# Two units of a Strassen-type product by turns in eight banks, with side work in small steps

## The chip, the cores and the metric

The kernel runs on one core of one Trainium2 chip. The metric is the device time of one execution in microseconds (us): the median of the runs.

## What is computed

```python
def _attn_ref(q_l, k_l, v_l, q_g, k_g, v_g):      # 4 sequences, 8 heads, 512 local + 32 global rows, 64 wide
    ...                                           # sliding-window attention with global rows
def _moe_ref(x, w_in, w_out):                     # 2304 x 512, hidden 2048
    h = np.maximum(x @ w_in, 0.0)
    return (h * h @ w_out).astype(np.float32)
def _moe2_ref(x, w1, w2, w3, w_out):              # hidden 1024
    a = x @ w1
    b = x @ w2
    h = a * b @ w3
    return (h @ w_out).astype(np.float32)
def reference(...):
    x = attn_out.transpose(0, 2, 1, 3).reshape(B * S, H * D)
    x = _moe_ref(x=x, **moe_kwargs)
    return _moe2_ref(x=x, **moe2_kwargs)
```

## The kernel before

Activations lie transposed: 128 partitions hold a slice of the 512 features, and the rows of the four sequences (p = 0 to 3, 544 rows each) lie along the free side. Precision comes from splitting each float32 operand in a high and a low part (`split_operand`, `split_w`: a cast on ScalarE to the high part, a subtraction on DVE for the low one) and from three matmuls (`PASSES`) for each product. ScalarE is called ACT and GpSimd POOL in the rows, DMA issues go by SP's queue.

Attention and the first MLP come first, in blocks of 256 or 288 rows; beside them the weights are converted from their 64-bit form (`conv`). The second MLP multiplies w3 by w_out once into one matrix of 1024 x 512 (`w_unit`, stored to `w_d`), so that two products are left.

The *first product* (the stage of the change) is a and b and their elementwise product, `ab_unit(p, f)`: a unit takes 128 hidden columns of w1 together with those of w2 as two block rows (a above, b below), the two halves of the 512 inputs as the inner blocks, and the two halves of a sequence's rows (272 each, `NP`) as block columns. This 2 x 2 block product is done with seven products in place of eight (Winograd's form, `ORDER` = 1, 6, 5, 7, 4, 2, 3). Each product is six matmuls of 272 columns (two inner blocks, three passes), so a unit is 42 and the 32 units are 1344. `Blocks.step(i)` issues product i (L709) and the operations that read its bank: after product 1 a copy by ScalarE (L726), after 6, 7, 4 and 3 additions by DVE (L729, 731, 733, 736, 739); `ab_unit.done` adds the elementwise product (L845 on DVE after product 2, L847 on GpSimd after 3). Products 7, 2 and 3 accumulate onto the banks of 6, 1 and 5 (`BANK`). A unit takes four of the eight PSUM banks, so the units alternate between two sets.

f = 4 h + j: the units j and 4 + j give slice j of the two halves of the hidden layer, which are the inner blocks of the last product; they share a staging tile `rs` (two buffers), in which GpSimd makes the sums that the last product needs (L848, one for h = 0, three for h = 1), and which goes to DRAM (`q_d`, L856).

The operands of a sequence come from `load_x2` (one load), four subtractions of 544 columns (L754) and 14 splits (L745 cast, L119 subtraction) in `operands`. The tile ring for them has seven places of two and one from the ring `u1`, so one operand of the next sequence can lie ready while the old ones are in use. They are issued for units 4 and 6 and then between the products of a sequence's last unit.

The weights of units FIRST are split when they are converted; the sums and values of those of LATE go to DRAM and come back (`late_w12`, 16 casts at L414 and 16 subtractions at L119), and are then kept in ring `u2` up to the last sequence, which begins with them. There the combined matrix Wv takes their place (`load_wv`, `late_blocks`); its sums are made by GpSimd in the second sequence (`sum_wv`). The *last product*, `y_unit(p, s)`, runs two units by turns, each product being 12 matmuls; its rows are read back from `q_d` (`load_r`, L893) and split (`split_r`).

The order of the instructions of each engine is made by a scheduler when the program is built: an instruction that is traced later may be placed ahead of an earlier one of the same engine, where its inputs and buffers allow it. `tc.keep_in_program_order(i)` ties i behind what was traced before it on its engine. `merge` spreads lists of steps over others.

Of the kernel before, what the change touches and what calls it, by code (L numbers as in the profile page):

```python
# [74 lines left out]
NP = S // 2  # L75

# [8 lines left out]
def attention_mlp(ctx: ExitStack, tc: tile.TileContext, kq0, kq, vw, wts, mask, ident, out_d):  # L85
    nc = tc.nc
# [326 lines left out]
    def split_w(t, cols, raw):  # L413
        nc.scalar.copy(t[:, 0, cols], raw)  # L414
        split_lo(nc.vector, t[:, 1, cols], raw, t[:, 0, cols])
# [15 lines left out]
    def split_blocks(key, n, x, s, tag):  # L431

        p, q, r = (unit(tag) for _ in range(3))
        split_w(p, slice(0, 512), x[:, 0])
        split_w(q, slice(0, 512), s[:, 0])
        split_w(r, slice(0, 512), s[:, 1])
        if n % 2 == 0:
            half_t[tag] = unit(tag)
        h, at = half_t[tag], 256 * (n % 2)
        split_w(h, slice(at, at + 256), x[:, 1, 256:])  # L440
        blocks_w[key] = {1: (p, 0), 2: (p, 256), 5: (q, 0), 6: (q, 256), 7: (r, 0), 3: (r, 256), 4: (h, at)}

    def conv_c(n):
        _, b, m = mid_t.pop(n)
        if n >= PAIRED:
# [4 lines left out]
            if u == 1:  # L450
# [5 lines left out]
                else:  # L456
                    split_blocks(FIRST[k - 4], k, x, s, "u1")
# [286 lines left out]
    def split_operand(t, raw):  # L744
        nc.scalar.copy(t[:, 0], raw)  # L745
        split_lo(nc.vector, t[:, 1], raw, t[:, 0])
        return t

    def operands(p, x, t1, t2):
# [3 lines left out]
        def make(i):  # L753
            sub = lambda o, a, c: nc.vector.tensor_tensor(out=o, in0=a, in1=c, op=ALU.subtract)  # L754
            if i == 0:
                sub(t1, b(0, 1), b(0, 0))
                sub(t2, b(1, 1), t1)
                return
            if i == 7:
                sub(t1, b(1, 1), b(0, 1))  # L760
            if i == 4:
                sub(t2, t2, b(1, 0))
            raw = {1: b(0, 0), 6: t2, 5: t1, 7: t1, 4: t2, 2: b(1, 0), 3: b(1, 1)}[i]
            spare = (7 * p + ORDER.index(i)) % 8 == 7
            xo["x", p, i] = [
                split_operand(unit("u1")[:, :, :NP] if spare else parts(NP), raw[:, k]) for k in range(2)
            ]

        return {i: lambda i=i: make(i) for i in (0, *ORDER)}
# [26 lines left out]
    def ops_early(d):  # L796
        if d == 0:
            first_ops()
            ops[0][0]()
        if d < 2:  # L800
            ops[0][ORDER[d]]()
# [18 lines left out]
    main += [lambda i=i: ops[0][i]() for i in ORDER[2:]] + [end]  # L820
# [5 lines left out]
    stage = {}  # L826

    def ab_unit(p, f):
# [7 lines left out]
        def out(m, n):  # L836
            if (m, n) == (1, 1):
# [189 lines left out]
```

## Time and profile before

| | us |
|---|---|
| median of 3 runs | 905.8 (905.39 to 906.59) |
| profiled execution | 909.1 |
| its span | 907.3 |
| PE busy in it | 853.8 (94%) |
| DVE busy | 589.8 (65%) |
| ScalarE busy | 493.6 (54%) |
| GpSimd busy | 209.0 (23%) |
| first product (L709) on PE from | 615.8 |

PE's busy time is that of matmuls, whose ends are modelled; "idle before" is the time in which an engine had nothing to run ahead of that row, with what ended it. A row of a timeline merges like instructions that follow one another. PEclk is the granted clock of TensorE as a share of full speed, 2.4 GHz.

### The profile page before, as it was taken

The numbers are of one execution on the slowest core, as the hardware profiler recorded it, in microseconds if no ns is written. First come the engines' busy times: TensorE is split into PE (matmuls) and PEld (weight loads), VectorE is DVE, ScalarE is ACT, GpSimd is POOL, SyncE is SP. The second block draws the span as 40 slices with busy tenths as digits, with TensorE's granted clock in tenths as the row PEclk, the third lists the DMA queues.
The fourth block names the chain that finished last, engine by engine and source line by source line (L and its number), as shares of the span: only waits on it lengthen the run. The fifth ranks groups of instructions, "written<-read, shape, count | busy, mean of one in ns | idle before, by whom it ended". The sixth has DMA issues, their size and how long they took to land.

```text
span 907.3 us, 17924 instructions
## 1 busy us (share of the span) xinstructions
PE 853.8 (94%) x6664; PEld 802.3 (88%) x6664; DVE 589.8 (65%) x1617; ACT 493.6 (54%) x1317; POOL 209.0 (23%) x254
## 2 busy tenths in 40 slices
PE   5799999999999999899998999999989998989998
PEld 3578898899999999899898998998979898889998
DVE  6998775876576465456444346898484847677762
ACT  6886675766576577777555446775020203234550
POOL 1432000000010022222222112210754443442000
PEclk9889999999999999999999999999999998999999
DMA  6743525133232156466454549576473333637762
GB/s 231 242 156 102 170 62 156 53 124 100 97 120 74 48 182 206 156 226 204 147 188 139 187 162 326 190 241 228 150 243 111 112 107 103 222 126 256 250 231 74
DMA packets 85303, 147.51 MB, mean 163 GB/s; under 512 B 6112, under 2 KB 58464, under 8 KB 85216
## 3 DMA queue, kind: packets, MB, share of 16 engines
q1 hardware_dynamic: 85216, 146.37, 49.0%
q8 instruction: 52, 0.85, 0.4%
q14 instruction: 35, 0.29, 0.1%
HBM read 100.07 MB, written 46.27 MB: 161 GB/s over the span
## 4 chain that ended last, share of the span: by engine, by line
PE 47%; DMA 20%; DVE 16%; ACT 11%; issue 4%; SPq 1%; POOL 1%; ACTq 0%; DVEq 0%; POOLq 0%
PE m L709 16%; DMA wraw<-in_wts 11%; PE h L130 10%; PE x L130 7%; DMA rl<-q_d 4%; PE o L124 3%; DVE hl L119 3%; DVE u L119 3%; DVE wt L404 3%; PE sc L124 3%; PE tp L278 3%; PE acc L539 2%; ACT wt L391 2%; ACT u L414 2%; DMA x2l<-x_d 2%
## 5 line engine op out<-in xcount | busy, mean ns | idle before, releaser
L130 PE MATMUL h<-hl,u 128*128 128x288 f32 (+1 forms) x1536 | 232.1, 295 | 7.0 <-ACT r L503 3.1
L130 PEld LDWEIGHTS h<-hl,u 128*128 128x128 f32 x1536 | 206.9, 191 | 15.3 <-ACT r L503 5.5
L709 PE MATMUL m<-hl,u 128*128 128x272 f32 x1488 | 202.8, 294 | 14.1 <-DVE r L731 6.1
L709 PEld LDWEIGHTS m<-hl,u 128*128 128x128 f32 x1488 | 194.9, 193 | 17.8 <-DVE r L731 7.2
L539 PE MATMUL acc<-hl,u 128*128 128x256 f32 (+1 forms) x960 | 138.9, 290 | 3.1 <-ACT hl L504 1.7
L539 PEld LDWEIGHTS acc<-hl,u 128*128 128x128 f32 x960 | 128.8, 190 | 6.1 <-DVE hl L119 2.4
L459 POOL TENSOR_TENSOR wt<-wt 128x512 int32<-128x512 int32 x56 | 76.2, 1361 | 227.9 <-DVE wt L404 132.0
L119 DVE TENSOR_TENSOR hl<-r,hl 128x288 fp32r<-128x288 f32 (+1 forms) x128 | 65.5, 519 | 63.0 <-ACT r L510 62.6
L130 PE MATMUL x<-hl,u 128*128 128x288 f32 (+1 forms) x576 | 89.2, 297 | 0.2 <-ACT u L414 0.2
L391 ACT ACTIVATE wt<-wraw 128x512 f32<-128x512 f32 x72 | 48.3, 673 | 63.0 <-DMA wraw<-in_wts 62.5
L130 PEld LDWEIGHTS x<-hl,u 128*128 128x128 f32 x576 | 76.9, 189 | 4.5 <-issue 1.9
L709 PE MATMUL m<-u,u 128*128 128x272 f32 x528 | 73.9, 289 | 4.1 <-DVE r L729 2.2
L709 PEld LDWEIGHTS m<-u,u 128*128 128x128 f32 x528 | 68.2, 188 | 6.2 <-DVE r L729 2.6
L201 ACT ACTIVATE p<-p,st 128x256 f32<-128x256 f32 x128 | 64.2, 506 | 9.9 <-DVE st L197 9.8
L119 DVE TENSOR_TENSOR u<-wt,u 128x512 fp32r<-128x512 f32 x56 | 39.8, 712 | 44.3 <-ACT u L414 43.6
L503 ACT ACTIVATE r<-h 128x288 f32<-128x288 f32 (+1 forms) x128 | 49.5, 391 | 32.9 <-PE h L130 32.3
L726 ACT COPY r<-m 128x272 f32<-128x272 f32 x40 | 15.3, 383 | 81.3 <-PE m L709 62.3
L197 DVE CUSTOM_DVE_ANT_0 p<-sc,mask_sb 128x256 f32<-128x256 f32 x128 | 46.9, 417 | 19.1 <-PE sc L124 18.9
L230 POOL CAST qgp<-kq_hl 64x32 fp32r<-64x32 f32 x48 | 16.4, 343 | 178.1 <-PE sg L130 149.8
L404 DVE SCALAR_TENSOR_TENSOR wt<-wraw,wt 128x512 int32<-128x512 int32 x72 | 54.5, 756 | 1.4
L504 ACT ACTIVATE hl<-r 128x288 fp32r<-128x288 f32 (+1 forms) x128 | 54.0, 430 | 2.0
L848 POOL TENSOR_TENSOR rs<-rs 128x272 f32<-128x272 f32 x64 | 52.8, 835 | 3.3
(97 smaller groups left out, 1203.5 us busy)
## 6 DMA issues: line engine op xcount, KB each, us to landing
wraw<-in_wts SPq DMA_DIRECT2D x72, 512.0 KB, 3.7
q_d<-rs SPq DMA_DIRECT2D x16, 952.0 KB, 4.5
rl<-q_d SPq DMA_DIRECT2D x12, 1088.0 KB, 5.7
v_f<-in_vw SPq DMA_DIRECT2D x24, 256.0 KB, 3.0
xs_d<-hl SPq DMA_DIRECT2D x16, 288.0 KB, 3.2
hl<-xs_d SPq DMA_DIRECT2D x16, 288.0 KB, 4.0
x2l<-x_d SPq DMA_DIRECT2D x4, 1088.0 KB, 7.5
out<-u SPq DMA_DIRECT2D x16, 272.0 KB, 3.4
```

What stands on the lines that cost most here:

```text
L119: eng.tensor_tensor(out=lo, in0=raw, in1=hi.bitcast(F32), op=ALU.subtract)
L124: m = mm(o, w, x, start=start, stop=stop)
L130: mm(o, w, x, start=(k == 0), stop=(k == len(terms) - 1))
L201: nc.scalar.activation(p[:, n, :], p[:, n, :], AF.Exp, bias=least[:, n : n + 1], scale=-1.0, accum_out=sums[:, n, 0:1],)
L391: first = nc.scalar.activation(t[0].bitcast(F32), raw[:, :, 1].bitcast(F32), AF.Copy, scale=2.0**-112)
L404: nc.vector.scalar_tensor_tensor(out=b, in0=raw[:, :, 1], scalar=-(1 << 31), in1=a, op0=ALU.bitwise_and, op1=ALU.bitwise_or)
L459: nc.gpsimd.tensor_tensor(out=b, in0=b, in1=m, op=ALU.add)
L503: nc.scalar.activation(r, h, AF.Relu)
L504: nc.scalar.activation(g[:, 0], r, AF.Square)
L539: mm(acc[d], w[:, a, 128 * d : 128 * (d + 1)], g_t[f][:, b], start=(f + k == 0), stop=(f + k == 9),)
L709: mm(o, w, x, start=(i in (1, 6, 5, 4) and k == 0), stop=(k == len(terms) - 1), skip_group_check=(i in (2, 7, 3)),)
L848: sub = lambda o, a, c: nc.gpsimd.tensor_tensor(out=o, in0=a, in1=c, op=ALU.subtract)
```

## The change

Two units (0 and 4, 1 and 5, 2 and 6, 3 and 7 of a sequence, in the same order of pairs) run product by product by turns: product 1 of both, then 6 of both, and so on. Between the products of a pair `between(p, m, k)` issues the side work in fixed small steps, by tables: AHEAD (steps of the next sequence's operands by pair m and product k), LATE_W and LATE_V (steps of the late weights in the first and of Wv in the last sequence). The DVE subtractions of the splits and the operands' subtractions (from the second sequence on) are tied to program order. The operands get ten places, two of them from the ring `xb`. The third result of a unit goes to the staging tile instead of a temporary; the stores to `q_d` are issued three products into the next pair. Loads for the last product are issued earlier and use `rs` buffers too. Of the diff, lines without change are left out.

```diff
@@ -73,6 +73,14 @@
+PLACES = 10
+AHEAD = ((0, 0, 0, 0, 0, 0, 0), (1, 0, 1, 0, 1, 0, 1), (1, 0, 1, 0, 1, 0, 1), (2, 1, 2, 0, 2, 1, 2))
+LATE_W = ((2, 1, 1, 0, 2, 1, 1), (1, 1, 1, 1, 1, 1, 1), (1, 1, 1, 0, 1, 0, 0))
+LATE_V = ((1, 0, 0, 0, 0, 0, 0), (2, 1, 2, 0, 2, 1, 1), (2, 1, 2, 0, 2, 1, 2), (0, 0, 0, 0, 0, 0, 0))
@@ -410,9 +418,13 @@
     def unit(tag, dtype=F32R):
-    def split_w(t, cols, raw):
+    def split_w(t, cols, raw, held=False):
-        split_lo(nc.vector, t[:, 1, cols], raw, t[:, 0, cols])
+        s = nc.vector.tensor_tensor(
+            out=t[:, 1, cols], in0=raw, in1=t[:, 0, cols].bitcast(F32), op=ALU.subtract
+        )
+        if held:
+            tc.keep_in_program_order(s)
@@ -428,17 +440,22 @@
-    def split_blocks(key, n, x, s, tag):
-        p, q, r = (unit(tag) for _ in range(3))
-        split_w(p, slice(0, 512), x[:, 0])
-        split_w(q, slice(0, 512), s[:, 0])
-        split_w(r, slice(0, 512), s[:, 1])
-        if n % 2 == 0:
-            half_t[tag] = unit(tag)
-        h, at = half_t[tag], 256 * (n % 2)
-        split_w(h, slice(at, at + 256), x[:, 1, 256:])
-        blocks_w[key] = {1: (p, 0), 2: (p, 256), 5: (q, 0), 6: (q, 256), 7: (r, 0), 3: (r, 256), 4: (h, at)}
+    def split_blocks(key, n, x, s, tag, held=False):
+        t = []
+        def third(raw):
+            t.append(unit(tag))
+            split_w(t[-1], slice(0, 512), raw, held)
+        def last():
+            if n % 2 == 0:
+                half_t[tag] = unit(tag)
+            (p, q, r), h, at = t, half_t[tag], 256 * (n % 2)
+            split_w(h, slice(at, at + 256), x[:, 1, 256:], held)
+            blocks_w[key] = {1: (p, 0), 2: (p, 256), 5: (q, 0), 6: (q, 256), 7: (r, 0), 3: (r, 256), 4: (h, at)}
+        return [*(lambda raw=raw: third(raw) for raw in (x[:, 0], s[:, 0], s[:, 1])), last]
     def conv_c(n):
@@ -454,7 +471,8 @@
-                    split_blocks(FIRST[k - 4], k, x, s, "u1")
+                    for f in split_blocks(FIRST[k - 4], k, x, s, "u1"):
+                        f()
@@ -741,32 +759,53 @@
-    def split_operand(t, raw):
+    def split_operand(t, raw, held=True):
-        split_lo(nc.vector, t[:, 1], raw, t[:, 0])
+        s = nc.vector.tensor_tensor(out=t[:, 1], in0=raw, in1=t[:, 0].bitcast(F32), op=ALU.subtract)
+        if held:
+            tc.keep_in_program_order(s)
+    room = {}
+    def place(n):
+        n, at = divmod(n, PLACES)
+        if at < 7:
+            return [parts(NP) for _ in range(2)]
+        if at == 7:
+            return [
+                unit("u1").rearrange("p a c -> p (a c)")[:, : 2 * NP].rearrange("p (a c) -> p a c", a=2)
+                for _ in range(2)
+            ]
+        if at == 8:
+            room[0] = sb.tile([128, 2, 2, 2, NP], F32R, tag="xb", name="xo", bufs=2)
+        return [room[0][:, at - 8, k] for k in range(2)]
     def operands(p, x, t1, t2):
-        def make(i):
-            sub = lambda o, a, c: nc.vector.tensor_tensor(out=o, in0=a, in1=c, op=ALU.subtract)
-            if i == 0:
-                sub(t1, b(0, 1), b(0, 0))
-                sub(t2, b(1, 1), t1)
-                return
+        def sub(o, a, c):
+            s = nc.vector.tensor_tensor(out=o, in0=a, in1=c, op=ALU.subtract)
+            if p > 0:
+                tc.keep_in_program_order(s)
+        raw = {1: b(0, 0), 6: t2, 5: t1, 7: t1, 4: t2, 2: b(1, 0), 3: b(1, 1)}
+        def split(i, k):
+            if k == 0:
+                xo["x", p, i] = place(7 * p + ORDER.index(i))
+            split_operand(xo["x", p, i][k], raw[i][:, k], p > 0)
+        steps = [lambda: sub(t1, b(0, 1), b(0, 0)), lambda: sub(t2, b(1, 1), t1)]
+        for i in ORDER:
-                sub(t1, b(1, 1), b(0, 1))
+                steps.append(lambda: sub(t1, b(1, 1), b(0, 1)))
-                sub(t2, t2, b(1, 0))
-            raw = {1: b(0, 0), 6: t2, 5: t1, 7: t1, 4: t2, 2: b(1, 0), 3: b(1, 1)}[i]
-            spare = (7 * p + ORDER.index(i)) % 8 == 7
-            xo["x", p, i] = [
-                split_operand(unit("u1")[:, :, :NP] if spare else parts(NP), raw[:, k]) for k in range(2)
-            ]
-        return {i: lambda i=i: make(i) for i in (0, *ORDER)}
+                steps.append(lambda: sub(t2, t2, b(1, 0)))
+            steps += [lambda i=i, k=k: split(i, k) for k in range(2)]
+        return steps
     def in_staging():
@@ -796,9 +835,8 @@
     def ops_early(d):
-            ops[0][0]()
-        if d < 2:
-            ops[0][ORDER[d]]()
+        for _ in range(4 if d == 0 else 2 if d == 1 else 0):
+            ops[0].pop(0)()
@@ -817,13 +855,18 @@
-    main += [lambda i=i: ops[0][i]() for i in ORDER[2:]] + [end]
+    main += [lambda n=n: [ops[0].pop(0)() for _ in range(n)] for n in (2, 3, 3, 2, 2)] + [end]
-    stage = {}
+    stage, made = {}, []
+    def store_r():
+        for p, j in made:
+            nc.sync.dma_start(out=q_d[:, :, p, j], in_=stage[p, j][:, 1:])
+        made.clear()
     def ab_unit(p, f):
@@ -834,11 +877,9 @@
         def out(m, n):
-            if (m, n) == (1, 1):
-                return temp()
-            return stage[p, j][:, (1, 0, 6, 7)[2 * h + n]]
+            return stage[p, j][:, ((1, 0, 2), (6, 7, 5))[h][n + m * n]]
         def done(u, i):
@@ -853,7 +894,7 @@
-                    nc.sync.dma_start(out=q_d[:, :, p, j], in_=stage[p, j][:, 1:])
+                    made.append((p, j))
@@ -868,17 +909,35 @@
     def sum_wv(j):
-        nc.sync.dma_start(out=sums_d[4 + j], in_=add_up(load_wv(j), "u2", nc.gpsimd))
-    def late_blocks(key, n, x):
-        s = unit("u2", F32)
-        nc.sync.dma_start(out=s, in_=sums_d[n])
-        split_blocks(key, n, x, s, "u2")
-    def late_w12(k):
+        sums = add_up(load_wv(j), "u2", nc.gpsimd)
+        return lambda: nc.sync.dma_start(out=sums_d[4 + j], in_=sums)
+    late_t = {}
+    def late_load(key, n, load):
+        late_t[n] = (load(), unit("u2", F32))
+        nc.sync.dma_start(out=late_t[n][1], in_=sums_d[n])
+    def late_split(key, n, k):
+        if k == 0:
+            late_t[n] = split_blocks(key, n, *late_t[n], "u2", True)
+        late_t[n][k]()
+    def load_w12(k):
-        late_blocks(LATE[k], k, x)
+        return x
+    def late_steps(todo, order=(0, 1, None, 2, None, 3, None, None)):
+        load = [lambda t=t: late_load(*t) for t in todo]
+        steps, n = [], 0
+        for k in order:
+            if k is not None:
+                steps.append(load[k])
+                continue
+            steps += [lambda t=todo[n], k=k: late_split(*t[:2], k) for k in range(4)]
+            n += 1
+        return steps
     def next_x(p):
@@ -889,7 +948,11 @@
     def load_r(p, o):
-            t = sb.tile([128, 2, 4, NP], F32, tag="xb", name="rl", bufs=2)[:, :n]
+            if o < 4:
+                t = sb.tile([128, 2, 4, NP], F32, tag="xb", name="rl", bufs=2)[:, :n]
+            else:
+                t = rs.tile([128, 8, NP], F32, tag="rs", name="rl", bufs=2)
+                t = t.rearrange("p (k j) n -> p k j n", k=2)[:, :n]
@@ -905,37 +968,51 @@
+    late_v = late_steps([(("v", j), 4 + j, lambda j=j: load_wv(j)) for j in range(4)], (0, 1, None, None, 2, 3, None, None))
+    late_w = late_steps([(LATE[k], k, lambda k=k: load_w12(k)) for k in range(4)])
+    def take(steps, n):
+        for f in steps[:n]:
+            f()
+        del steps[:n]
+    def between(p, m, k):
+        if k == 3:
+            store_r()
+            take(sums_v, len(sums_v))
+        if p + 1 < B:
+            if m == 0 and k == 0:
+                next_x(p + 1)
+            take(ops[p + 1], AHEAD[m][k])
+            if p == 0 and m < 3:
+                take(late_w, LATE_W[m][k])
+        else:
+            if m == 2 and k in (0, 3):
+                load_r(0, 2 * k // 3)
+            take(late_v, LATE_V[m][k])
+            if m == 3 and k in (1, 4):
+                split_r(0, ORDER[k // 4])
+        if p == 1 and k == 0:
+            sums_v.append(sum_wv(m))
+    sums_v = []
+    late_w.pop(0)()
     for p in range(B):
-        for n, f in enumerate(order):
-            box = []
-            if n == 1:
-                main.append(lambda p=p: next_x(p + 1))
-            if n in (4, 6) and p + 1 < B:
-                main.append(lambda p=p, i=(0, 1)[n // 5]: ops[p + 1][i]())
-            if p == 1 and n % 2 == 0:
-                main.append(lambda j=n // 2: sum_wv(j))
-            if p == B - 1 and n in (2, 3, 4, 5):
-                main.append(lambda j=n - 2: late_blocks(("v", j), 4 + j, load_wv(j)))
-            if p == B - 1 and n == 4:
-                main.append(lambda: load_r(0, 0))
-            if p == B - 1 and n == 6:
-                main.append(lambda: split_r(0, 1))
-            if p == B - 1 and n == 7:
-                main.append(lambda: split_r(0, 6))
-            for i in ORDER:
-                if i == 1:
-                    main.append(lambda box=box, p=p, f=f: (box.append(ab_unit(p, f)), box[0].step(1)))
-                else:
-                    main.append(lambda box=box, i=i: box[0].step(i))
-                if n == 7 and p + 1 < B and i != 3:
-                    main.append(lambda p=p, i=ORDER[ORDER.index(i) + 1]: ops[p + 1][i]())
-            if p == B - 1 and n == 7:
-                for o in (2, 4, 6):
-                    main.append(lambda o=o: load_r(0, o))
-                    for i in ORDER[o : o + 2]:
-                        main.append(lambda i=i: split_r(0, i))
-    merge(main, ([lambda k=k: late_w12(k) for k in range(4)], 0, 30))
+        for m in range(4):
+            units = [ab_unit(p, f) for f in order[2 * m : 2 * m + 2]]
+            for k, i in enumerate(ORDER):
+                for u in units:
+                    u.step(i)
+                between(p, m, k)
+    store_r()
+    for o in (4, 6):
+        load_r(0, o)
+    for i in ORDER[2:]:
+        split_r(0, i)
+    for o in (0, 2, 4, 6):
+        load_r(1, o)
     def y_unit(p, s):
@@ -969,9 +1046,9 @@
-            if o % 2 == 0:
-                load_r(p + 1, o)
+            if o in (1, 3, 5, 6):
+                load_r(p + 2, o - o % 2)
```

## Rows read from the trace of the kernel before

**Rows 1.** Busy time by stretch; columns: window, length, each engine's busy us (operations), PEclk, DMA.

```profile
622.00:640.00 18.00, 16.14 (x123) 15.33 (x122) 14.25 (x33) 5.37 (x15) 5.87 (x8) 1.00 0.64 225
656.00:676.00 20.00, 16.01 (x124) 15.33 (x123) 18.21 (x36) 6.31 (x17) 11.97 (x15) 1.00 0.68 214
706.00:722.00 16.00, 14.25 (x105) 13.26 (x105) 15.21 (x33) 5.32 (x16) 6.13 (x7) 1.00 0.30 99
751.00:773.00 22.00, 19.02 (x130) 18.66 (x129) 17.07 (x36) 7.77 (x19) 7.73 (x9) 0.84 0.28 96
773.00:812.00 39.00, 34.00 (x241) 33.18 (x240) 25.91 (x57) 11.93 (x27) 14.60 (x18) 0.91 0.50 159
812.00:832.00 20.00, 18.36 (x146) 18.08 (x145) 14.04 (x36) 9.00 (x28) 7.07 (x9) 1.00 0.76 262
832.00:904.00 72.00, 70.72 (x562) 69.64 (x560) 43.49 (x120) 30.76 (x93) 0.00 (x0) 1.00 0.59 197
```

**Rows 2.** Timeline of PE; columns: start us, length us, engine, line, operation, count, idle before.

```profile
681.16 0.91 PE L709 MATMUL m<-u,u 128*128 128x272 f32 x6
...
702.63 0.90 PE L709 MATMUL m<-u,u 128*128 128x272 f32 x6
...
758.96 7.33 PE L709 MATMUL m<-hl,u 128*128 128x272 f32 x36 [2.98 <-ACT hl L745]
...
781.01 5.54 PE L709 MATMUL m<-hl,u 128*128 128x272 f32 x30 [1.54 <-ACT r L726]
...
787.13 4.77 PE L709 MATMUL m<-hl,u 128*128 128x272 f32 x36
...
800.81 6.31 PE L709 MATMUL m<-hl,u 128*128 128x272 f32 x36 [2.77 <-DVE r L731]
```

**Rows 3.** Timeline of DVE, third change of sequence and the last sequence.

```profile
749.99 0.44 DVE L731 TENSOR_TENSOR r<-r,m 128x272 f32<-128x272 f32 x1 [1.86 <-PE m L709]
...
751.99 0.79 DVE L119 TENSOR_TENSOR u<-t,u 128x272 fp32r<-128x272 f32 x2
...
753.39 0.72 DVE L754 TENSOR_TENSOR t<-x2l 128x544 f32<-128x544 f32 x1
754.02 2.88 DVE L119 TENSOR_TENSOR hl<-t,hl 128x272 fp32r<-128x272 f32 x3
756.82 1.29 DVE L754 TENSOR_TENSOR t<-t,x2l 128x544 f32<-128x544 f32 x1
758.04 0.43 DVE L119 TENSOR_TENSOR hl<-t,hl 128x272 fp32r<-128x272 f32 x1
...
768.14 0.69 DVE L119 TENSOR_TENSOR u<-u,u 128x512 fp32r<-128x512 f32 x1
...
797.04 2.43 DVE L119 TENSOR_TENSOR u<-u,u 128x512 fp32r<-128x512 f32 x2
```

**Rows 4.** Timelines of GpSimd (first row) and ScalarE in the same stretch and after.

```profile
754.82 2.71 POOL L848 TENSOR_TENSOR rs<-rs 128x272 f32<-128x272 f32 x3
...
758.20 0.74 ACT L745 CAST hl<-t 128x272 fp32r<-128x272 f32 x2 [3.26 <-DVE t L754]
...
779.53 1.14 ACT L414 CAST u<-u 128x512 fp32r<-128x512 f32 x2 [2.23 <-DMA u<-sums_d]
...
829.73 2.34 ACT L745 CAST u<-rl 128x272 fp32r<-128x272 f32 x7 [4.38 <-DMA rl<-q_d]
```

**Rows 5.** Weight casts, 500 to 640 us (ns; first, last start); DMA issues from 610 (landing us).

```profile
L414 ACT CAST u<-u x32: 393/610/637, 571.6 to 625.3; 128x512 fp32r<-128x512 f32 x24, 128x256 fp32r<-128x256 f32 x8
...
q_d<-rs SPq DMA_DIRECT2D x16, 952.0 KB, 4.5
...
u<-sums_d SPq DMA_DIRECT2D x6, 512.0 KB, 4.5
```

**Rows 6.** GpSimd's busy time in the first and the second sequence.

```profile
622.00:665.00 43.00, 24.14 (x31) 1.00 0.61 206
665.00:708.00 43.00, 19.28 (x25) 1.00 0.45 154
```

## Prediction

> **What bounds the kernel now.** I read the busy time of each engine in stretches first, then the lists of PE's groups in the same stretches, then the timelines of PE, DVE, ScalarE and GpSimd at the places where PE stands still. Nothing before 622 us is changed on PE, so the question is the time from there to the end at 907.3 us. PE sets the pace: a unit of 42 matmuls takes 5.37 us in the undisturbed stretch (702.63 - 681.16 = 21.47 us for four units) [rows 2]. What can be won is the time in which PE waits or runs at the lower clock, and the windows show where it is [rows 1]: window less PE busy gives 1.86 us at the start (622 to 640), 3.99 and 1.75 at the first two changes of sequence (656 to 676, 706 to 722), 2.98 at the third (751 to 773), 5.00 in the last sequence (773 to 812), 1.64 where the last product begins (812 to 832) and 1.28 in all the rest. Sum 18.5 us. Behind three of the waits the granted clock is below 1 [rows 1] and the same 36 matmuls that take 4.77 us at 787.13 [rows 2] take 7.33 and 6.31; 30 take 5.54 where 30/36 of 4.77 is 3.98. That is 2.56 + 1.54 + 1.56 = 5.7 us more. So 24.2 us are open: 2.98 + 2.56 + 3.99 + 1.75 = 11.3 at the changes of sequence, 5.00 + 3.10 = 8.1 in the last sequence, 1.86 at the start, 2.9 in the last product.
>
> Why PE waits there is seen on DVE. At 754 us it works through the new sequence's operands without a gap; ScalarE waits 3.26 us for a DVE subtraction before it can cast the next one [rows 3, 4], and PE waits for that cast at 758.96 [rows 2]. In the last sequence ScalarE waits 2.23 us for a weight sum on its way from DRAM, with DVE and PE behind it [rows 4]; at 829.73 ScalarE has waited 4.38 us for a load of the product's rows.
>
> **The change part by part.** *Two units in turn.* The 1344 matmuls stay, so at 0.128 us each the stage costs the same when it never waits. What changes is the distance from a result to the matmul that needs its bank read. One product of six matmuls is 5.37/7 = 0.77 us. Product 7 adds onto the bank of product 6 once DVE has read it: one product (5) lies between, 0.77 us; with two units it is three, 2.3 us. Product 3 onto the bank of 5: from two products to five, 3.8 us. The price is that both units' banks are full, and the next pair begins in the banks of this one: its first product needs the bank that DVE's product line has read after product 2, with three products (2.3 us) between. The slack of about 2.3 us covers up to five ordinary DVE adds of 0.35 to 0.47 us (five in 2.00 us) [rows 3]. The last product already runs with two units and eight banks, and has 1.28 us of waits in 72 [rows 1]; that is the nearest row for the new form.
>
> *Operands in small steps.* Four subtractions and 14 splits per sequence stay; they now run 0, 4, 4 and 10 in the four pairs of the sequence before, not 14 splits in and after its last unit. Ten places instead of eight let three operands lie ready. Splits and subtractions cost, start to start, 0.35 us (two in 0.79, so lengths overlap by 0.08) and 0.64 (0.72 for one) alone, and 0.96 (three in 2.88) and 1.22 (756.82 to 758.04) while GpSimd works [rows 3, 4]. DVE's adds from PSUM keep their time. Per pair the adds are 2 x (2.00 + 0.35) = 4.7 us of the pair's 10.74.
>
> *Late weights.* Their splits (16 casts, 16 subtractions) ran before the stage had well begun: the last cast of this line before 640 us starts at 625.3 [rows 5]. Pinned in program order on DVE they move into the first sequence. Alone they cost 12 x 0.60 + 4 x 0.35 = 8.6 us (0.69 for one less the overlap; 1.18 beside GpSimd: two in 2.43) [rows 3]. That is the change's cost, and its cover is DVE's idle time in that sequence. Ledger, first sequence: 4 x 4.7 + 8.6 + (14 x 0.35 + 4 x 0.64 = 7.5) = 34.9 of 43.0 us. GpSimd was busy 24.1 and 19.3 of 43 us in the first two [rows 6], so about half of the 16.1 us of SBUF work is disturbed: 12 x 0.58/2 + 4 x 0.61/2 + 14 x 0.61/2 + 4 x 0.58/2 = 10.1 more, 45.0 us: DVE is 2.0 us over PE. Bounds: none disturbed, 0; nearly all, 10. I take 3, since the second pair alone has six splits of late weights and four steps. (GpSimd's sums of the final weights are issued at each pair of the second sequence, with their load and their store on SP's queue; today free buffers let them run in the first, inside its 24.1 us. Where they run adds nothing to PE's work, and in the second sequence DVE has room for them.)
>
> Sequences two and three: 31 of 43 us, no loss on average, but their last pairs hold ten steps: 4.7 + 8 x 0.35 + 2 x 0.64 + half of (8 x 0.61 + 2 x 0.58) = 11.8 of 10.74; the slack takes 1.1. I take 0.3 each, bounds 0 and 2. Last sequence: the splits of the final weights (8.6 us) lie in its second and third pair, with loads one step earlier. In the third pair two loads are issued only after the pair's first products and the first split follows one product of each unit later, 1.5 us, while such a sum needs 4.5 us to land [rows 5]; unless the free buffers let the loads go sooner, ScalarE waits up to 3 us, and on DVE the pinned subtraction holds what follows it, the adds whose banks PE wants. I take 1.5, bounds 0 and 5 (3 us plus lost clock).
>
> *Rows of the last product* come from DRAM a whole step of the loop sooner, into four buffers. Of 2.9 us 0.8 stay; bounds 0 and 3, the upper because the loads now stand on SP's queue ahead of the output stores, and a store that is late holds a buffer. *Start:* the first pair gives PE two units' products to begin with, and DVE has no late weights there; 0.7 of 1.86 stay, bounds 0 and 2. *Third result in the staging tile,* not in a temporary: no instruction more; ScalarE's waits for a temporary go. *Stores three products later:* GpSimd's six operations per pair, 0.9 us each at worst (2.71 for three) [rows 4], end 5.4 us into the next pair, the store goes at about 6.1 and lands 4.5 later [rows 5]; the buffer is wanted 16 us into it. Nothing.
>
> Sum of what stays: 3 + 0.6 + 1.5 + 0.8 + 0.7 = 6.6, and 1 us for waits that I don't foresee: 24.2 - 7.6 = 16.6 us won. The profiled execution took 909.1 us, a span of 907.3 and 1.8 around it; it is 3.3 above the median of 905.8. The gain taken from its span leaves 890.7; from the median, 889.2. I forecast 889.
>
> *A rule that speaks against it.* The rows show that a DVE split beside GpSimd takes 0.96 us and not 0.35 [rows 3, 4], and the change puts GpSimd's six operations of a pair one behind the other, against the first half of the next pair. The Trainium skill (SBUF — State Buffer, section "SBUF: two separate sides") says that the port pair of the two is an exclusive lock: the loser waits for the whole operation. By that alone a disturbed split would cost 0.35 + 0.9 = 1.25 us, the 34 operations of the first sequence, half of them disturbed, would cost 15.3 us more and not 10.1, DVE would be 7 us over PE and not 2, and the time would be 894. The trace agrees in kind (DVE's operations from PSUM keep their length), but 0.96 is less than the two lengths together; I go by the row.
>
> **The rivals.** *A: DVE stays the bound, in the first sequence and with the last weights.* The upper bounds of these terms, 10 + 2 + 5, with 0.8 + 0.7 + 1 give 19.5 that stay: 4.7 won, 901; a milder case is 896. For it: pinned steps can't be put off when an add is urgent. Against: undisturbed, DVE has 8 us to spare even in the first sequence. *B, slower: saturation.* If all two-input SBUF work met GpSimd, the first sequence would need 18.8 + 12 x 1.18 + 18 x 0.96 + 4 x 1.22 = 55.1 us, 12.1 over; the last pairs of the next two 4.7 + 8 x 0.96 + 2 x 1.22 = 14.8, 4.1 over each; two pairs of the last 4.7 + 6 x 1.18 + 2 x 0.96 = 13.7, 3 over each. 26.3 us, with some 1.5 us of lower clock behind each of four waits 32: 8 us slower, 914. It decides from about four fifths disturbed; against it stands GpSimd's share of 56% at most [rows 6]. *C: the products aren't run in turn after all,* since the matmuls themselves are pinned to no order; PE then keeps its short slack and waits about as now, 905 or 906. *D: nothing is left but the last waits:* 2 us stay, 883.
>
> **How the numbers follow.** Forecast (883 to 895) 0.70, A 0.14, B 0.08, C 0.06, D 0.02. A measurement of this kernel can tell about 0.2%, 1.8 us, from no change. Faster by more: 0.70 + 0.14 + 0.02 + a little of C = 0.87; within: 0.05; slower: B, 0.08. The range 882 to 901 holds forecast, A and D; B and C are left out.
>
> **What would show it.** Right: in the profile after, PE's timeline has rows of six matmuls by turns for both units; the waits at the three changes of sequence fall from 8.7 us together to under 2; the granted clock stays at 1 from 622 us on; late-weight subtractions appear between 625 and 655 us; DVE is busy over 90% in the first sequence and PE's waits left there name DVE's adds. Wrong: waits of PE of 1 us and more for DVE in the second and third pair of the first sequence (A, B); ScalarE waiting for weight sums in the last sequence's third pair with PE still behind it (A); any new window with a clock below 0.9.

## The result

The changed kernel takes 882.8 us (median of 4 runs, 881.9 to 886.2) against 905.6 before: a ratio of 0.9754, 95% interval 0.9725 to 0.9782. Its profiled execution has a span of 884.4 us, 22.9 less than 907.3. The forecast was 889.

The first view is the busy time of the engines by stretch, here by sequence (first, second, third, last) and the last product; the columns are those of [rows 1].

```profile
623.30:664.60 41.30, 40.12 (x314) 39.19 (x312) 37.89 (x77) 11.32 (x29) 18.16 (x19) 1.00 0.33 108
664.60:707.20 42.60, 42.47 (x339) 42.19 (x337) 28.77 (x65) 8.56 (x25) 30.83 (x40) 1.00 0.67 225
707.20:749.50 42.30, 42.30 (x336) 42.17 (x337) 28.77 (x67) 6.68 (x20) 20.82 (x24) 1.00 0.36 125
749.50:794.30 44.80, 42.80 (x340) 42.13 (x338) 35.46 (x74) 17.44 (x41) 21.23 (x24) 1.00 0.64 208
794.30:881.00 86.70, 85.91 (x684) 85.16 (x684) 60.43 (x157) 39.26 (x116) 5.37 (x6) 1.00 0.62 224
```

Window less PE busy is 1.18, 0.13, 0.00, 2.00 and 0.79 us: 4.1 us, where [rows 1] gave 18.5. The granted clock is 1.00 in every stretch; in [rows 1] it fell to 0.84 and 0.91. DVE is busy 37.9 of 41.3 us in the first sequence, and GpSimd (fifth engine) 18.2 us there and 30.8 in the second.

The timeline of PE, where it still waits, and three rows one pair apart:

```profile
651.80 1.76 PE L727 MATMUL m<-hl,u 128*128 128x272 f32 x12 [0.53 <-DVE r L747]
654.06 10.72 PE L727 MATMUL m<-hl,u 128*128 128x272 f32 x84 [0.49 <-DVE r L749]
...
675.25 0.97 PE L727 MATMUL m<-xo,u 128*128 128x272 f32 x6
...
685.83 0.96 PE L727 MATMUL m<-xo,u 128*128 128x272 f32 x6
...
696.35 0.96 PE L727 MATMUL m<-xo,u 128*128 128x272 f32 x6
...
780.78 1.78 PE L727 MATMUL m<-hl,u 128*128 128x272 f32 x12 [1.00 <-ACT r L744]
783.40 1.76 PE L727 MATMUL m<-hl,u 128*128 128x272 f32 x12 [0.84 <-DVE r L749]
...
822.47 1.79 PE L727 MATMUL m<-u,u 128*128 128x272 f32 x12 [0.45 <-DVE u L757]
```

The waits at the changes of sequence are gone. What is left is DVE's adds in the third pair of the first sequence, a copy by ScalarE and an add at 781 to 783, and one wait in the last product. And a pair takes 10.58 and 10.52 us, where two units took 10.74 [rows 2]: PE is faster also where it waited for nothing that was listed.

Behind the wait at 780.78 stands the load that the prediction named. ScalarE's and DVE's timelines and GpSimd's (the rows with ACT, DVE and POOL):

```profile
776.94 1.45 ACT L422 CAST u<-u 128x512 fp32r<-128x512 f32 x3 [1.97 <-DMA u<-sums_d]
...
779.20 0.93 ACT L422 CAST u<-u 128x512 fp32r<-128x512 f32 x2 [0.49 <-DMA u<-w_d]
...
780.35 0.37 ACT L744 COPY r<-m 128x272 f32<-128x272 f32 x1
...
781.11 1.89 DVE L423 TENSOR_TENSOR u<-u,u 128x512 fp32r<-128x512 f32 x3
...
789.66 3.58 POOL L889 TENSOR_TENSOR rs<-rs 128x272 f32<-128x272 f32 x4
...
790.60 3.29 DVE L764 TENSOR_TENSOR u<-rl,u 128x272 fp32r<-128x272 f32 x4
```

ScalarE waits 1.97 us for a weight sum and 0.49 for a weight on their way from DRAM; the copy that frees PE's bank (L744) comes after them, at 780.35. Then DVE runs three tied subtractions of the final weights (1.89 us), and PE waits 0.84 us for the add behind them (783.40). Below, four DVE splits take 3.29 us beside four operations of GpSimd in 3.58. By the single records only the first three meet GpSimd, 0.95 us each from start to start; the fourth begins after GpSimd's last and takes 0.43.

One more thing is read from the program's instruction list, not from the trace: PE doesn't run the products in the order of the source, in either kernel. The scheduler has mixed neighbouring units. In steady state (unit : product):

```
before  6:6 5:2 4:3 6:4 6:1 5:7 6:5 | 7:6 6:2 5:3 7:4 7:1 6:7 7:5 | ...
after   11:7 12:7 13:6 11:3 13:4 14:6 13:1 12:3 14:4 13:5 14:1 13:2 14:5 14:2 | 13:7 14:7 15:6 ...
```

As far as tile names tell, the timeline agrees: in the second sequence product 1 reads its operand from u and products 6 and 5 from xo, and from 685.83 on PE's rows after are 6 matmuls with xo, 12 with hl, 6 with xo, 6 with u, 12 with hl, as in the list (6, 3 4, 6, 1, 3 4). So the kernel before already ran units between one another, and in the kernel after a pair isn't run by turns. Most of the experiments are about that.

### The profile page after: what moved, and what is told of

Its sections match the earlier page's. It is cut to its first block, busy times and chain, and to the rows that moved or that the text cites. A ratio compares the mean times of both kernels' runs of the same rounds, so it can differ in the third digit from the quotient of the medians.

```text
span 884.4 us, 17923 instructions
## 1 busy us (share of the span) xinstructions
PE 846.0 (96%) x6664; PEld 797.8 (90%) x6664; DVE 590.6 (67%) x1617; ACT 494.1 (56%) x1317; POOL 212.9 (24%) x254
## 5 line engine op out<-in xcount | busy, mean ns | idle before, releaser
L727 PE MATMUL m<-hl,u 128*128 128x272 f32 x1296 | 172.5, 288 | 3.2 <-DVE r L749 1.3
L727 PEld LDWEIGHTS m<-hl,u 128*128 128x128 f32 x1296 | 165.5, 188 | 4.8 <-DVE r L749 2.1
L727 PE MATMUL m<-u,u 128*128 128x272 f32 x528 | 71.1, 287 | 0.7 <-DVE u L757 0.5
L205 DVE CUSTOM_DVE_ANT_0 p<-sc,mask_sb 128x256 f32<-128x256 f32 x128 | 46.9, 417 | 19.2 <-PE sc L132 18.9
L744 ACT COPY r<-m 128x272 f32<-128x272 f32 x40 | 15.4, 384 | 76.4 <-PE m L727 76.3
L889 POOL TENSOR_TENSOR rs<-rs 128x272 f32<-128x272 f32 x64 | 56.4, 892 | 2.7
```

Source lines behind the costliest of these rows:

```text
L205: nc.vector.tensor_tensor_reduce(out=p[:, n, :], in0=sc[:, n, :], in1=mask_sb[:, 2 * part + n, :], scale=-SCALE, scalar=3.0e38, op0=ALU.ad ...
L727: mm(o, w, x, start=(i in (1, 6, 5, 4) and k == 0), stop=(k == len(terms) - 1), skip_group_check=(i in (2, 7, 3)),)
L889: sub = lambda o, a, c: nc.gpsimd.tensor_tensor(out=o, in0=a, in1=c, op=ALU.subtract)
```

## Experiments

All times are medians; ratios are to runs of the kernel before on the same chip.

**1. Ties and tables.** The kernel after without ties to program order:

```diff
-        if held:
-            tc.keep_in_program_order(s)
...
-            if p > 0:
-                tc.keep_in_program_order(s)
```

> The kernel after without any tie to program order; same tables, same turns. If the fixed order is what keeps DVE's adds in time: 888 or more, with waits of PE for DVE back at the changes of sequence. If the tables alone do it: 881 to 885. If the ties cost (a tied step holds the adds behind it, rival A): faster, 879 to 881.

Measured: 894.7 us, 0.9894 (0.9862 to 0.9926). The same without ties, and with the side work in lumps:

```diff
-AHEAD = ((0, 0, 0, 0, 0, 0, 0), (1, 0, 1, 0, 1, 0, 1), (1, 0, 1, 0, 1, 0, 1), (2, 1, 2, 0, 2, 1, 2))
+AHEAD = ((0,) * 7, (0,) * 7, (2, 0, 0, 0, 0, 0, 0), (2, 0, 0, 4, 4, 3, 3))
-LATE_W = ((2, 1, 1, 0, 2, 1, 1), (1, 1, 1, 1, 1, 1, 1), (1, 1, 1, 0, 1, 0, 0))
-LATE_V = ((1, 0, 0, 0, 0, 0, 0), (2, 1, 2, 0, 2, 1, 1), (2, 1, 2, 0, 2, 1, 2), (0, 0, 0, 0, 0, 0, 0))
+LATE_W = ((4, 0, 0, 0, 5, 0, 0), (5, 0, 0, 0, 5, 0, 0), (0,) * 7)
+LATE_V = ((0,) * 7, (5, 0, 0, 0, 5, 0, 0), (5, 0, 0, 0, 5, 0, 0), (0,) * 7)
...
-    def late_steps(todo, order=(0, 1, None, 2, None, 3, None, None)):
+    def late_steps(todo, order=(0, None, 1, None, 2, None, 3, None)):
...
```

> The kernel after, with the units by turns as they are, but the side work in lumps where the kernel before had it (the next sequence's two first subtractions at the third pair, two splits at the fourth, the other 14 steps in its second half; each block of late or final weights in one lump) and nothing tied to program order. If the turns give DVE's adds the slack that matters (the prediction's first step), the time stays within 3 us of the kernel after: 883 to 886. If spreading the side work is what took the waits away, the 8.7 us of waits at the changes of sequence and the 5 us in the last sequence come back, with lost clock: 895 to 903.

Measured: 896.2 us, 0.9909 (0.9882 to 0.9937). And in lumps, but with the ties:

> The kernel after with the side work in lumps (as in the run with lumps) but tied to program order. The runs without ties stand at 895 to 896 with either table, and their waits lie at the same places, so the tables seem to act through the ties alone. If it is the ties that pay, 884 to 890 here too; if it takes small steps and ties together, 900 or more, because a lump of five tied weight steps or four operand steps now holds every tied step behind it and delays DVE's adds by 3 us and more.

Measured: 893.8 us, 0.9856 (0.9829 to 0.9883), between the two expected cases.

Small steps alone give nothing over lumps that can be told (894.7 and 896.2; the intervals overlap). Ties alone, in lumps, give little: 2 us by the medians, 5 us by the ratios, whose intervals just touch. Both together give 882.8. In lumps with ties PE waits at each change of sequence:

```profile
670.02 5.75 PE L727 MATMUL m<-hl,u 128*128 128x272 f32 x32 [2.09 <-ACT hl L763]
...
715.36 1.02 PE L727 MATMUL m<-hl,u 128*128 128x272 f32 x6 [2.25 <-DVE rs L886]
...
763.20 5.48 PE L727 MATMUL m<-hl,u 128*128 128x272 f32 x42 [1.91 <-ACT hl L763]
```

PE's timelines of the two kernels without ties, steps and then lumps, show why the table is idle there:

```profile
640.75 24.45 PE L725 MATMUL m<-hl,u 128*128 128x272 f32 x180 [2.50 <-DVE r L745]
...
677.75 1.02 PE L725 MATMUL m<-hl,u 128*128 128x272 f32 x6 [1.64 <-DVE r L745]
...
780.08 2.21 PE L725 MATMUL m<-hl,u 128*128 128x272 f32 x12 [1.84 <-DVE r L747]
```

```profile
637.15 24.29 PE L725 MATMUL m<-hl,u 128*128 128x272 f32 x180 [2.51 <-DVE r L745]
...
673.88 1.02 PE L725 MATMUL m<-hl,u 128*128 128x272 f32 x6 [1.64 <-DVE r L745]
...
776.68 2.21 PE L725 MATMUL m<-hl,u 128*128 128x272 f32 x12 [1.85 <-DVE r L747]
```

The same waits at nearly the same distance from one another: without ties the scheduler places the side work by itself, wherever the source has it. Behind the three waits the granted clock falls, in the kernel with steps to 0.57, 0.64 and 0.63 over 4.0 to 4.8 us (640.75 to 644.75, 677.75 to 682.50, 780.00 to 784.60), most of it the lower of the two levels. Some 40 matmuls start 227 ns apart there and not 125, 4 us in all; PE's listed waits up to 800 us are 6 us more than in the kernel after (8.9 and 2.9). DVE's timeline of the kernel with untied steps, ahead of the first of these waits:

```profile
636.35 1.60 DVE L762 TENSOR_TENSOR xo<-t,xo 128x272 fp32r<-128x272 f32 x2
637.88 1.28 DVE L786 TENSOR_TENSOR t<-x2l 128x544 f32<-128x544 f32 x1
639.08 1.27 DVE L786 TENSOR_TENSOR t<-t,x2l 128x544 f32<-128x544 f32 x1
640.28 0.77 DVE L745 TENSOR_TENSOR r<-r,m 128x272 f32<-128x272 f32 x2
```

It runs the next sequence's splits and subtractions in one go as early as the second pair, beside GpSimd (two splits in 1.60 us, 1.28 and 1.27 for a subtraction), and the add that PE needs (L745) follows at 640.28. That is the jam of the kernel before [rows 3], at another place.

**2. Turns.** The kernel after with the units of a pair one after the other in the source:

```diff
-            for k, i in enumerate(ORDER):
-                for u in units:
-                    u.step(i)
-                between(p, m, k)
+            for t, (u, i) in enumerate([(u, i) for u in units for i in ORDER]):
+                u.step(i)
+                if t % 2 == 1:
+                    between(p, m, t // 2)
```

> The kernel after with the two units of a pair one after the other in the source; side work in the same small steps, tied to program order, at the same share of the pair. If spreading is what matters: 883 to 887, of which up to 3.5 us for the second interval of 230 ns (125 elsewhere) that the kernel before shows once in each of its 32 units. If the turns matter most: 895 or more, since the tied steps now stand against adds with half the slack.

Measured: 880.8 us, 0.9747 (0.9716 to 0.9778). The turns in the source are worth nothing: the tied steps hold the time without them, and the short interval that I expected back didn't come back. Then three kernels whose matmuls are tied to the order of the source, so that PE runs what the source says (the lines that set `turn` are left out):

```diff
-            mm(
+            ins = mm(
                 o, w, x, start=(i in (1, 6, 5, 4) and k == 0), stop=(k == len(terms) - 1),
                 skip_group_check=(i in (2, 7, 3)),
             )
+            if turn[0]:                      # within the first product
+                tc.keep_in_program_order(ins)
```

on the kernel before (unit by unit),

> The kernel before with the matmuls of the first product tied to the order of the source: unit after unit, products 1, 6, 5, 7, 4, 2, 3, which is what the prediction took the kernel before to do. Read from the program, PE's order in the kernel before is another: the scheduler has products of three neighbouring units between one another (6 of unit n+1, 2 of n, 3 of n-1, 4 of n+1, 1 of n+1, 7 of n, 5 of n+1). If that mix bought nothing, 904 to 908. If it already gave part of the slack that the prediction put down to the turns, slower: 0.2 us and more in each of 32 units, 912 to 925.

on the kernel after (by turns),

> The kernel after with the matmuls of the first product tied to the source's order, so that PE really runs the two units product by product (1 1 6 6 5 5 7 7 4 4 2 2 3 3), as the prediction described it; side work as in the kernel after. If the slack of 2.3 us that the prediction worked out is right, 881 to 885, with hardly a wait beside those of the kernel after. If the scheduler's own mix is better than the turns, 888 or more.

and on the kernel after with units one after another.

> Units one after another in the source (as in the run with units in sequence) and the matmuls tied to that order: 1 6 5 7 4 2 3, unit by unit; side work in small steps, tied. It has the short distance of one product, 0.77 us, between 6 and 7. Beside the run in turns it prices the slack by itself: if the step on slack is right, 0.2 to 0.4 us more in each of 32 units and waits where side steps stand between, 895 to 910; if the slack is worth nothing once side work is spread, within 2 us of the run in turns.

Measured: 922.6 (1.0201, 1.0163 to 1.0239), 883.9 (0.9744, 0.9719 to 0.9768) and 896.1 us (0.9888, 0.9857 to 0.9919). PE's timeline by turns, rows of twelve matmuls (one product of both units) one pair apart, and then unit by unit:

```profile
644.85 16.70 PE L729 MATMUL m<-hl,u 128*128 128x272 f32 x132 [1.07 <-DVE r L751]
661.39 1.67 PE L729 MATMUL m<-u,u 128*128 128x272 f32 x12
...
671.87 1.66 PE L729 MATMUL m<-u,u 128*128 128x272 f32 x12
...
682.34 1.66 PE L729 MATMUL m<-u,u 128*128 128x272 f32 x12
...
692.84 1.66 PE L729 MATMUL m<-u,u 128*128 128x272 f32 x12
```

```profile
696.89 0.92 PE L729 MATMUL m<-u,u 128*128 128x272 f32 x6
...
718.01 1.01 PE L729 MATMUL m<-u,u 128*128 128x272 f32 x6 [1.42 <-DVE r L751]
...
729.29 1.02 PE L729 MATMUL m<-u,u 128*128 128x272 f32 x6 [0.39 <-DVE r L751]
...
781.89 3.38 PE L729 MATMUL m<-hl,u 128*128 128x272 f32 x18 [2.29 <-DVE r L751]
```

By turns a pair takes 10.48, 10.47 and 10.50 us and PE never waits over three pairs. Unit by unit it waits for the add of DVE that reads product 6 (L751), onto whose bank product 7 adds, and six matmuls behind such a wait take 1.02 us and not 0.92. So the slack that the prediction worked out is real, 12.2 us between these two, if PE follows the source; but the scheduler's mix gives as much, in the kernel before too: tied to unit by unit that one loses 17 us, and its longest waits (4.30 and 4.72 us) are for the add of product 6.

**3. The other parts.** The late weights' subtractions not tied:

```diff
-            late_t[n] = split_blocks(key, n, *late_t[n], "u2", True)
+            late_t[n] = split_blocks(key, n, *late_t[n], "u2", isinstance(key, tuple))
```

> The kernel after, with the late weights' subtractions in the first sequence not tied. They go back to the end of the first MLP, where DVE in the kernel after is busy 55 to 77% from 600 to 620 us. The prediction put the cost of tying them at 3 us; PE's waits in the kernel after between 625 and 665 us are 1.1 us and with their follow-up gaps 2 us. If the prediction's term is right in kind, 1 to 3 us faster than the kernel after: 879 to 882. If the scheduler's own place for them is worse, as for the other side work, 884 or more.

Measured: 884.0 us, 0.9747 (0.9696 to 0.9797), runs from 878.4 to 889.3: no difference that can be told. Eight places for the operands in place of ten:

```diff
-PLACES = 10
+PLACES = 8
-AHEAD = ((0, 0, 0, 0, 0, 0, 0), (1, 0, 1, 0, 1, 0, 1), (1, 0, 1, 0, 1, 0, 1), (2, 1, 2, 0, 2, 1, 2))
+AHEAD = ((0,) * 7, (1, 0, 0, 0, 1, 0, 0), (1, 0, 0, 0, 1, 0, 0), (2, 2, 3, 3, 2, 2, 0))
```

> The kernel after with eight places for the operands, as in the kernel before, and the table set to what eight places allow: two subtractions in the second pair, one operand's two splits in the third, 14 of the 18 steps after the first six products of the fourth. Ties and turns stay. If the ten places carry part of the gain, DVE needs 4.7 + 12 x 0.35 + 2 x 0.64 and some 4 us of disturbance, 14 us in a pair of 10.5, at each of three changes of sequence: 2 to 3 us each, 888 to 892. If small tied steps are enough wherever they stand, 882 to 885.

Measured: 884.4 us, 0.9770 (0.9717 to 0.9823): no difference that can be told either. DVE was to be 2 to 3 us over in each last pair; PE waited 0.85 us at the first change of sequence and 0.65 and 0.37 at the third. That the lag is made up in the pair behind, which has no side steps, is argued and not shown. The third result back in a temporary, on the kernel with units in sequence:

```diff
         def out(m, n):
+            if (m, n) == (1, 1):
+                return temp()
```

> Units one after another in the source, tied small steps (the run with units in sequence, 880.8), and the third result back in a temporary that GpSimd's product frees, as in the kernel before. The prediction put the move to the staging tile at nothing but ScalarE's waits, 18.9 us in all in the kernel before, of which 1.5 reached PE. If that is right, 881 to 884; if the temporaries held the pace, 886 or more.

Measured: 887.8 us, 0.9805 (0.9758 to 0.9853), against 880.8 and 0.9747 without this edit. Who waited for whom (us in total, times, longest) in that kernel from 620 to 800 us, and PE's longest wait:

```profile
ACT r L744 <- POOL rs L890: 22.6, 8, 6.2
```

```profile
659.49 1.77 PE L727 MATMUL m<-hl,u 128*128 128x272 f32 x12 [0.45 <-ACT r L744]
...
689.26 2.52 PE L727 MATMUL m<-hl,u 128*128 128x272 f32 x18 [1.69 <-ACT r L744]
```

ScalarE's copy waits 22.6 us in all for GpSimd to free a temporary, as it did in the kernel before (18.9), and PE waits for that copy, 1.69 us at 689.26. PE's pace changes too, where no wait is listed. Products 5 and 6 of two units, one unit apart, with the temporary and then without:

```profile
675.12 1.76 PE L727 MATMUL m<-xo,u 128*128 128x272 f32 x12
...
680.46 1.77 PE L727 MATMUL m<-xo,u 128*128 128x272 f32 x12
```

```profile
680.11 1.66 PE L727 MATMUL m<-xo,u 128*128 128x272 f32 x12
...
685.37 1.67 PE L727 MATMUL m<-xo,u 128*128 128x272 f32 x12
```

A unit takes 5.34 us with the temporary, as in the kernel before, and 5.26 without. PE's order is another as well: with the temporary one whole product (hl) stands between product 1 (u) and products 5 and 6, as in the list of the kernel before; without it, none or a part of one. So moving the third result is a part of the gain by itself, some 5 us by the two ratios (0.58% of 905; their intervals overlap by 0.2%, so the size is rough) and 7 by the medians, and it needs neither turns nor eight banks.

**4. Towards a better kernel.** Loads of the final weights earlier against their splits, and two splits of the last product's rows later, on the kernel with units in sequence and on the kernel after:

```diff
-LATE_V = ((1, 0, 0, 0, 0, 0, 0), (2, 1, 2, 0, 2, 1, 1), (2, 1, 2, 0, 2, 1, 2), (0, 0, 0, 0, 0, 0, 0))
+LATE_V = ((1, 0, 0, 0, 1, 0, 0), (1, 1, 2, 0, 2, 1, 2), (1, 0, 1, 1, 2, 2, 2), (0, 0, 0, 0, 0, 0, 0))
-            if m == 3 and k in (1, 4):
-                split_r(0, ORDER[k // 4])
+            if m == 3 and k in (3, 5):
+                split_r(0, ORDER[(k - 3) // 2])
```

> Units one after another in the source, tied small steps, with two tables changed: the loads of the final weights one product to three products earlier than their first split, the splits of the third pair a little later, and the two operands of the last product that are split in the last pair two products later, when GpSimd is done. The waits that this aims at (1.4 and 1.6 us for DVE near 790 and 802 us in the run with units in sequence) would go: 877 to 880 against 880.8; if they only move, 880 to 883.

> The kernel after with the same two tables changed. The waits it aims at: 1.0 us for ScalarE (itself waiting for a load) and 0.8 for DVE near 781 to 783 us, 0.4 near 794. If they go, 879 to 882 against 882.8; if they only move, 882 to 885.

Measured: 878.9 us, 0.9701 (0.9660 to 0.9742), and 882.9 us, 0.9757 (0.9716 to 0.9798). PE's waits of the first, which is the fastest kernel that was run, are all that its timeline lists from 650 us on:

```profile
716.08 1.15 PE L727 MATMUL m<-xo,u 128*128 128x272 f32 x7 [0.77 <-ACT r L744]
...
746.55 6.26 PE L727 MATMUL m<-hl,u 128*128 128x272 f32 x48 [0.17 <-DVE r L749]
...
787.63 9.22 PE L727 MATMUL m<-u,u 128*128 128x272 f32 x69 [0.24 <-DVE u L764]
...
817.51 3.23 PE L727 MATMUL m<-u,u 128*128 128x272 f32 x24 [0.99 <-DVE u L757]
```

The waits near 790 and 802 us in the kernel with units in sequence,

```profile
790.30 1.01 PE L727 MATMUL m<-hl,u 128*128 128x272 f32 x6 [1.37 <-DVE r L747]
...
802.57 1.79 PE L727 MATMUL m<-u,u 128*128 128x272 f32 x12 [1.57 <-DVE r L747]
```

have become 0.24 at 787.63; one in the last product has grown to 0.99. With the turns in the source the same edit moved them and won nothing. The interval of the fastest kernel and that of the kernel after overlap by a little, and so do those of the two kernels with units in sequence.

## Why the prediction was right, and where its steps were not

**What bounds the kernel.** Right. The time came back where PE waited: 18.5 us of waits became 4.1, and the lower clock, 5.7 us, is gone. That is 20.1 us of the 22.9; the rest is the next point.

**"The stage costs the same when it never waits."** This step failed. The stretch that was taken for undisturbed held a wait too short to be listed: a unit took 5.37 us [rows 2], half a pair now takes 5.26 to 5.29. Over 32 units that is about 3 us, which the sum didn't have. By the start times of the matmul records, the second of two matmuls follows the first by 230 ns and not 125 once in each unit of the kernel before; in the kernel after this happens about once in a pair, mostly with 170 to 180 ns. By the order given above, it is where product 6 of a unit enters the bank that product 7 of two units before has left, one product after it. The records agree: the first of the two matmuls starts 0.05 to 0.06 us after the end of DVE's add of product 7 (L731), the same distance as behind the listed waits for that add (672.72, 800.81). With the units in sequence it is the move of the third result that takes it away: with the temporary back, 5.34 us a unit are back, and the 230 ns behind the same add (L749 there).

**"Two units in turn."** The step on which the prediction put its weight first, and the wrong one. It took the kernel before to run unit by unit. It didn't: its scheduler had already mixed the units, and that mix was worth 17 us (922.6 against 905). The slack of 2.3 us was worked out rightly for the order of the source (883.9 against 896.1), but the turns in the source changed the time by nothing (880.8 without them). Rival C said that without real turns the time would stay near 905; PE runs no turns in the kernel after (the rows of six by turns that were to show it right aren't there), and the time fell.

**"Operands in small steps."** Right in place, and under-rated: the ties were booked as a cost only, as what holds an add behind a waiting step (rival A). They are what makes the table hold: 894.7 without ties, 893.8 with ties and lumps, 882.8 with ties and small steps, so 11 to 12 us rest on the two together by the medians (13 and 9 by the ratios, as the chips differ). The ten places, which the prediction counted in this step, have no share that can be told.

**Late weights, the ledger.** It gave DVE 45.0 us in the first sequence, 2 over PE, and a loss of 3. DVE was busy 37.9 us and PE waited 1.2 in that sequence, the start included. Two terms were too high: nearly all of GpSimd's sums of the final weights ran in the second sequence, so it was busy 44% in the first and not 56%, and fewer steps than half met it (of the 16 late subtractions 5 took 0.99 to 1.26 us, the others 0.41 to 0.69). The second sequence, with GpSimd busy 72% of the time, cost PE 0.13 us. Untied, the late weights cost and gain nothing (884.0). Rival B, saturation, needed four fifths of the steps disturbed and was far off.

**The last sequence.** 1.5 us (0 to 5) was set for the final weights' loads, and 2.0 us were measured in that sequence, 1.84 of it by the mechanism named: ScalarE waits for a sum and PE for the copy behind it (1.00), then for an add that tied subtractions hold (0.84). Here the term was good.

**Last product and start.** 0.8 was taken for the last product, 0.79 measured. For the start 0.7 was taken; PE's first listed wait of the stage is at 651.80, so it cost nothing that is listed. No run takes the earlier loads of the last product back, so that they won this is not shown by itself.

**The third result in the staging tile.** Booked at no gain beyond ScalarE's waits. It is worth 5 to 7 us: with the temporaries back, window less PE busy from 623 to 800 us is 6.2 us, and 2.1 without them (both with the units in sequence), and the pace gives the other 3 us. How a temporary comes to change the scheduler's order isn't shown.

**The rule of the skill.** By the Trainium skill (SBUF — State Buffer, section "SBUF: two separate sides") a split beside GpSimd was to cost 1.25 us, by an estimate from its rule and this kernel's lengths. It took 0.95 here and 0.96 in [rows 3], and the first sequence lost less than by either price; the forecast by the rows was nearer.

In sum, 7.6 us were to stay and 4.1 did; 3 us came from the pace. Both errors lie on the same side, and 6 us is what the forecast missed. The range and the direction held, with the gain put down to the wrong one of its parts: that the number came so near is in part luck. The ties with small steps (9 to 13 us) and the third result (5 to 7) carry most of the gain; neither was run alone on the kernel before, so whether the two simply add up isn't shown.

## What to carry to other kernels

When a scheduler places the instructions, read the order that it made before reasoning about distances in the source: here the order of the matmuls in the source moved nothing, and a tie to program order on the side steps moved 12 us. Cut side work of a busy second engine into steps smaller than the slack and tie them; small steps alone gave nothing here, ties alone at most 5 us of 14. A buffer that a slow engine frees (here a temporary read by GpSimd) is worth moving even when the waits put down to it are short.

## What was new of the hardware

Behind a wait of PE the second matmul starts 230 ns after the first and not 125, so six matmuls take 1.02 us and not 0.92 (unit by unit, at 729.29 and 696.89). The same 0.1 us is lost where the wait is too short to be listed: in the kernel before once in each unit, some 3 us over the stage that no view of idle time shows.
